# A fixed instruction order revised in a fused agent-attention and feed-forward kernel on one Trainium2 core

## The chip, the core and the metric

The kernel runs on one core of a Trainium2 chip. The metric is the device time of one launch in microseconds (us). The engines are named as in the profile: PE is TensorE (matmuls; PEld its weight loads), DVE is VectorE, ACT is ScalarE, POOL is GpSimd, and SP is SyncE, which issues the DMAs.

## The reference

Four batches of 12,480 rows of 128 go through an attention with 49 agents, and then, as 49,920 tokens, through a feed-forward layer. All is float32.

```python
def _attn_ref(q, k, v, agents):
    scale = 1.0 / np.sqrt(q.shape[-1])
    def sm(a, b):
        s = scale * (a @ b.transpose(0, 2, 1))
        s = s - s.max(-1, keepdims=True)
        e = np.exp(s)
        return e / (e.sum(-1, keepdims=True) + 1e-09)
    agent_v = sm(agents, k) @ v
    return sm(q, agents) @ agent_v

def _moe_ref(x, w_in, w_out):        # w_in: 128 x 2048, w_out: 2048 x 128
    h = x @ w_in
    g = h - np.tanh(h)
    return g @ w_out
```

## The kernel before, in words

The work has two parts, which the kernel runs beside each other.

**The feed-forward part** sets the pace. The product agent_v @ w_in (49 x 2048) is made once per batch, as a rounded part `awh` and a remainder `awl` (`project`, from L433). A batch is cut into 25 blocks of 500 tokens (the last of 480), which makes 100 blocks; two of them are a pair. Each block has eight steps (NCH // 2), each for 256 of the 2048 columns, so there are 800 steps, and sixteen positions (`pos`, 0 to 15) in a pair. For each step:

- the first product `m1` (L528): four matmuls into `h` (L533 with `awh`, L534 with `awl`); `h` has three buffers of two PSUM banks;
- `pre` (L540) on ScalarE: `y` = tanh (L543), then `z` = y squared (L545);
- `mul` (L549) on VectorE: `g` = h times z (L551);
- `high` (L579): `gh`, a rounded copy of `g`, on GpSimd (L584) or, for some steps, on ScalarE (L582);
- `low` (L587) on VectorE: `gl` = g minus gh (L589), the remainder;
- the second product `m2` (L592): six matmuls into the block's accumulator in PSUM, for each of two halves `wo_l` x `gh` (L602), `wo_h` x `gh` (L603), `wo_h` x `gl` (L604). In a plain step (all of block 0, and step PLAIN_PAIR of every even block) there is no `gh` and `gl`, and two float32 matmuls (L600) take their place.

Step k of the loop in `fast` (from L804) issues `squares(k + 1)`, the multiplication and rounding of step k, `low` of step k - 1, the second product of step k - 1, and the first product of step k + AHEAD.

**The attention part** is cut into jobs, which are Python generators. A job that has been started is moved on by one `yield` at the beginning of each step (L822 to L829), so what it issues there stands in front of that step's own multiplication on VectorE and behind the latest square on ScalarE (`hold`, L830).

- A q job (`q_softmax`, L477), one per pair, for the next pair: products of q and the agents (L487), their maximum on VectorE (L494), a copy on ScalarE (L495), the subtraction on GpSimd (L497), exp (L499), sums and division on VectorE (L501 to L504), a rounded copy `pp` on ScalarE (L507) and its remainder on GpSimd (L510). QGAPS says how many steps lie between these. Two jobs `q_transpose` (L515) then make `pT`, the operand of the first product; T0 and T1 are the positions at which they start.
- For the next batch: 13 key jobs (`scores`, L232: products L277, copy to SBUF on ScalarE L279, maximum on VectorE L280), `max_in` and `max_out`, 13 value jobs (`av`, L313: subtraction on GpSimd L321, exp L328, products L336, addition L348), `sums` and four parts of `project`. They start at the positions KS (VS for value jobs), three in a pair. In the step in which a value job starts, the rounding `high` goes to ScalarE, and the job's subtraction waits for that step's multiplication (`wait_for`), so that it takes the rounding's place on GpSimd. At position QLOW the rounding goes to ScalarE too, and the subtraction L510 of the q job, a step later, has its place.

All short PSUM results share two banks (`misc`), of which the running accumulator holds one.

The order on VectorE, GpSimd and TensorE is that in which the program issues the instructions (`issue_order`, L864 to L866). On ScalarE it is written out only up to the end of block 0; after that the compiler's scheduler places the instructions, within what they need and `hold`.

Of the kernel before, what the change touches and what calls it, by code (L numbers as in the profile page):

```python
# [24 lines left out]
A = 49  # L25
# [8 lines left out]
GT = 8  # L34
# [20 lines left out]
LATE = 3  # L55
KV = 3
VB = 4
PLAIN_PAIR = 6
PLAIN_EVERY = 2
NB = dict(y=2, z=2, g=4, gh=4, gl=3)  # L60
Q0 = 2
NV = 10
SPLIT = (8, 9, 11, 13)
AHEAD = 3
QL = 0
QS = 2
QGAPS = (1, 1, 0, 2, 1, 1, 1)
QLOW = 8
T0 = 11
T1 = 13  # L70
KS = (3, 5, 13)
VS = (1, 3, 11)


def width(n):
# [23 lines left out]
class Build:  # L99
# [95 lines left out]
    def phase1(self, b):  # L195
# [30 lines left out]
        def ahead(kind, load, g, depth):  # L226
            have = st.setdefault(kind, [])
            while len(have) < min(NG, g + depth):
                have.append(load(len(have)))
            return have[g]  # L230

        def scores(g):  # L232
            yield
            yield
            if g == 0:
                st["s"] = self.keep.tile([128, NG * (GT + 1) * A], F32, tag="s", name="s", bufs=1)
                if b == 0:
                    st["mxp"] = self.work.tile([128, A, 2 * NG], F32, tag="mxp", name="mxp", bufs=1)
                else:
                    st["mxp"] = st["s"][:, NG * GT * A :][:, : A * NG].rearrange("p (a g) -> p a g", g=NG)  # L240
                st["acc"] = self.small.tile([128, C + 1], F32, tag="acc", name="acc")
            n = tiles(g)
            kt = ahead("k", load_k, g, 1 if b == 0 else kb - 1)
            if b and g >= NG - vb:
                ahead("v", load_v, 0, g - NG + vb + 1)
            if b == 0:
                ps = self.ph.tile([128, 2, 512], F32, tag="h", name="h")
                for t in range(n):
                    nc.tensor.matmul(  # L249
                        ps[:, t // 4, (t % 4) * A2 : (t % 4 + 1) * A2],  # L250
                        kt[:, t, :],
                        self.ag[:, 0:2, :],
                        start=True,
                        stop=True,
                    )
                pv = ps[:, :, : 4 * A2].rearrange("p c (t a) -> p c t a", a=A2)[:, :, :, :A]
                for c in range(-(-n // 4)):
                    m = min(4, n - 4 * c)
                    sl = slice((g * GT + 4 * c) * A, (g * GT + 4 * c + m) * A)
                    nc.scalar.copy(st["s"][:, sl].rearrange("p (t a) -> p t a", a=A), pv[:, c, :m])  # L260
                banks = -(-n // 4)
                nc.vector.tensor_reduce(
                    st["mxp"][:, :, 2 * g : 2 * g + banks].rearrange("p a c -> p c a"),
                    pv[:, :banks, : min(4, n)].rearrange("p c t a -> p c a t"),
                    axis=AX.X,
                    op=ALU.max,
                )
                if g == EARLY - 1:
                    nc.vector.tensor_reduce(
                        st["mxp"][:, :, 2 * NG - 1], st["mxp"][:, :, : 2 * EARLY], axis=AX.X, op=ALU.max  # L270
                    )
                return
            ps = self.misc()
            for t in range(n):
                for r in range(0, 128, QUART):
                    to = ps[r : r + QUART, t * A : (t + 1) * A]
                    nc.tensor.matmul(to, kt[:, t, r : r + QUART], self.ag[:, b, :], start=True, stop=True)  # L277
            yield
            nc.scalar.copy(st["s"][:, g * GT * A : (g * GT + n) * A], ps[:, : n * A])  # L279
            nc.vector.tensor_reduce(  # L280
                st["mxp"][:, :, g],
                ps[:, : n * A].rearrange("p (t a) -> p a t", a=A),
                axis=AX.X,
                op=ALU.max,
            )

        def max_in():
            yield
# [98 lines left out]
        def sums():  # L387
            yield
            yield
            if b == 0:  # L390
                an, n = st["acc"], HALF + A
                nc.vector.tensor_copy(an[:n, :C], st["ps"][:n, :C])
# [32 lines left out]
        if b == 0:  # L425
            self.mb_at = lambda: st["mb_at"]
            self.k0 = lambda g: ahead("k", load_k, g, 1)
            self.v0 = lambda g: ahead("v", load_v, g, 1)
        jobs = [scores(g) for g in range(NG)] + [max_in(), max_out(), None]
        jobs += [av(g) for g in range(NG)] + [None] * (b > 0) + [sums()]  # L430
        return jobs + self.project(b, True)

    def project(self, b, bound):  # L433
        nc = self.nc
# [42 lines left out]
    def q_softmax(self, halves, qt, res, TT=TT, gaps=(1,) * 7):  # L477
# [16 lines left out]
        nc.vector.tensor_reduce(m[:TT], pv, axis=AX.X, op=ALU.max)  # L494
        nc.scalar.copy(ev, pv)  # L495
        yield from (None,) * gaps[2]
        nc.gpsimd.tensor_tensor(ev, ev, m[:TT, :, None].broadcast_to([TT, GT, A]), ALU.subtract)  # L497
        yield from (None,) * gaps[3]
        nc.scalar.activation(ev, ev, AF.Exp, scale=SCALE)  # L499
        yield from (None,) * gaps[4]  # L500
# [91 lines left out]
    def m2(self, acc, i, gh, gl, wf=None):  # L592
        nc = self.nc
        w = gh.shape[1] // 2
        for c in range(2):
            f = 2 * i + c
            x = slice(c * w, (c + 1) * w)
            first, last = f == 0, f == NCH - 1
            if gl is None:
                nc.tensor.matmul(acc[:, :w], wf[:, c * C : (c + 1) * C], gh[:, x], start=first, stop=last)  # L600
                continue
            nc.tensor.matmul(acc[:, :w], self.wo_l[:, f, :], gh[:, x], start=first, stop=False)  # L602
            nc.tensor.matmul(acc[:, :w], self.wo_h[:, f, :], gh[:, x], start=False, stop=False)  # L603
            nc.tensor.matmul(acc[:, :w], self.wo_h[:, f, :], gl[:, x], start=False, stop=last)  # L604

    def last_name(self):
        return self.nc.cur_bb.bb.instructions[-1].name
# [37 lines left out]
    def fast(self):  # L645
# [101 lines left out]
        run(rest0.pop(0))  # L747
        run(dec[0])
        live = []
        kq, nv = [], 0  # L750
        r1, r2, done = [], [], []
        acc, outs, hs, zs = {}, {}, {}, {}

        def start(gen):
            if gen is not None:
                next(gen)
                live.append(gen)
# [17 lines left out]
        def squares(k):  # L775
            if k < len(steps):
                zs[k] = self.pre(hs[k], width(steps[k][0]))
# [26 lines left out]
        for k, (n, i) in enumerate(steps):  # L804
# [2 lines left out]
            p = n // 2  # L807
            if n % NBLK == 0 and i == 0 and b + 1 < B:
                kq = self.phase1(b + 1)
                nv = len(kq) - NG - 1  # L810
            first = self.count()
            while done and done[0][1] < k - 1:
                finish(done.pop(0)[0])
# [14 lines left out]
                    pass  # L828
            live[:] = nxt  # L829
            self.hold(first, self.act_at, (ET.Activation,))  # L830
            squares(k + 1)
            values = nv - NG - 2 < len(kq) < nv
            begin = kq and n and pos in (VS if values else KS)
            by_act = values and begin and kq[0] is not None or p and pos == QLOW and p + 1 < npair
            product(k, by_act)
            low(1)
            mark = self.last_on(ET.DVE)
            if n == 0:
# [10 lines left out]
            out(k)  # L849
            if n == 0 and i == HP - 1:  # L850
                self.issue_order(ET.Activation, at)
            first_product(k + AHEAD)
            if p and p + 1 < npair:
                if pos == QL:
                    qt[p + 1] = self.q_load(q_src(p + 1))
                if pos == QS:
                    start(q_job(p + 1))
            if begin:
                start(kq.pop(0))
        low(0)  # L860
        out(len(steps))
        while done:
# [63 lines left out]
```

## Time and profile before

| | |
|---|---|
| runs | 2222.31, 2222.56, 2222.90 us (median 2222.56) |
| profiled execution | 2226.41 us, span of its instructions 2224.6 us, granted clock 0.996 |
| first multiplication of step 0 | 58.9 us from the span's start |
| last multiplication | 2213.3 us |
| GpSimd roundings (L584) | 656 of 1667 ns |
| ScalarE roundings (L582) | 87 of 1020 ns |

The page of the profile gives each engine's busy time; groups of instructions with their mean duration and the idle time of the engine before them, with what ended it; the waits of one engine for another; and a timeline. In a row such as "DVE s L280 <- ACT s L279: 68.4, 38, 2.6" VectorE's instruction of line 280, which writes the tile s, waited for ScalarE's instruction of line 279: 68.4 us in all, 38 times, at most 2.6. A timeline row has the start in us, the duration in us, the engine, the line, the operation, out<-in, sizes, the number of instructions merged into the row and, in brackets, how long the engine was idle before it and who ended that.

### The profile page before, as it was taken

How to read it: one execution, taken by the hardware profiler on the slowest of the kernel's cores; microseconds unless marked ns; L12 is line 12 of the kernel's file. 1: busy time of each engine (PE TensorE's matmuls, PEld its weight loads, DVE VectorE, ACT ScalarE, POOL GpSimd, SP SyncE). 2: the span in 40 equal slices, each digit the busy share in tenths (PEclk: the TensorE clock that was granted, in tenths of full speed). 3: DMA queues.
4: the chain of work that ended last, by engine and by line, in shares of the span. 5: the costliest groups of instructions: out<-in, count | busy, mean ns of one | idle time of the engine just before them, and what ended most of it. 6: DMA issues, size and time to landing. Idle time of an engine off the chain costs nothing.

```text
span 2224.6 us, 37436 instructions
## 1 busy us (share of the span) xinstructions
PE 2113.7 (95%) x14885; PEld 1627.5 (73%) x14885; DVE 1987.3 (89%) x2028; ACT 1896.3 (85%) x2184; POOL 1340.2 (60%) x809
## 2 busy tenths in 40 slices
PE   7889899999999999999999999999999999999998
PEld 7567677777766767777777667777777777777776
DVE  7888899899988889988998889989999999999998
ACT  3877789998878888999888878898988989989887
POOL 0355566666656556666566556665666766767766
PEclk9999999999999999999999999999999999999999
DMA  9111111211111111112001110121010010000000
GB/s 360 62 58 57 51 37 54 66 52 38 38 45 50 48 50 47 57 50 66 29 19 57 59 49 19 38 67 49 19 34 23 20 37 20 29 29 19 28 10 20
DMA packets 65352, 109.15 MB, mean 49 GB/s; under 512 B 3985, under 2 KB 44177, under 8 KB 65169
## 3 DMA queue, kind: packets, MB, share of 16 engines
q1 hardware_dynamic: 65168, 106.68, 14.6%
q8 instruction: 119, 1.95, 0.4%
q14 instruction: 65, 0.52, 0.1%
HBM read 81.10 MB, written 25.56 MB: 48 GB/s over the span
## 4 chain that ended last, share of the span: by engine, by line
PE 69%; DVE 13%; ACT 12%; issue 4%; POOL 2%; DMA 0%; POOLq 0%; SPq 0%; DVEq 0%; ACTq 0%
PE misc L604 13%; PE h L534 13%; PE h L533 13%; PE misc L602 12%; PE misc L603 11%; DVE gl L589 6%; ACT y L543 5%; DVE g L551 4%; ACT z L545 4%; PE misc L600 3%; PE misc L336 2%; POOL gh L584 1%; PE h L249 1%; PE misc L520 1%; DVE s L280 1%
## 5 line engine op out<-in xcount | busy, mean ns | idle before, releaser
L584 POOL TENSOR_SCALAR gh<-g 128x1000 fp32r<-128x1000 f32 (+1 forms) x656 | 1091.9, 1667 | 669.2 <-DVE g L551 633.9
L551 DVE TENSOR_TENSOR g<-h,z 128x1000 f32<-128x1000 f32 (+1 forms) x800 | 952.0, 1192 | 53.7 <-ACT z L545 45.3
L543 ACT ACTIVATE y<-h 128x1000 f32<-128x1000 f32 (+1 forms) x800 | 803.1, 1004 | 221.1 <-PE h L534 214.4
L589 DVE TENSOR_TENSOR gl<-g,gh 128x1000 fp32r<-128x1000 f32 (+1 forms) x743 | 927.0, 1248 | 35.4 <-POOL gh L584 29.0
L545 ACT ACTIVATE z<-y 128x1000 f32<-128x1000 f32 (+1 forms) x800 | 833.2, 1042 | 21.6 <-DVE g L551 0.8
L604 PE MATMUL misc<-gl,wo_h 128*128 128x500 f32 (+1 forms) x1486 | 602.1, 405 | 89.3 <-DVE gl L589 89.1
L533 PE MATMUL h<-pT,awh 98*128 98x500 f32 (+1 forms) x1600 | 644.8, 403 | 3.2 <-ACT awh L453 1.5
L534 PE MATMUL h<-pT,awl 98*128 98x500 f32 (+1 forms) x1600 | 623.2, 390 | 0.4 <-DVE awl L456 0.4
L602 PE MATMUL misc<-gh,wo_l 128*128 128x500 f32 (+1 forms) x1486 | 599.2, 403 | 0.0
L603 PE MATMUL misc<-gh,wo_h 128*128 128x500 f32 (+1 forms) x1486 | 577.1, 388 | 0.0
L604 PEld LDWEIGHTS misc<-gl,wo_h 128*128 128x128 f32 x1486 | 279.4, 188 | 229.4 <-DVE gl L589 175.1
L533 PEld LDWEIGHTS h<-pT,awh 98*128 98x128 f32 x1600 | 301.5, 188 | 79.2 <-issue 12.5
L534 PEld LDWEIGHTS h<-pT,awl 98*128 98x128 f32 x1600 | 304.0, 190 | 73.5 <-issue 11.3
L603 PEld LDWEIGHTS misc<-gh,wo_h 128*128 128x128 f32 x1486 | 281.3, 189 | 50.1 <-issue 2.2
L602 PEld LDWEIGHTS misc<-gh,wo_l 128*128 128x128 f32 x1486 | 279.9, 188 | 48.8 <-issue 6.6
L497 POOL TENSOR_TENSOR qe<-qe,qm 126x392 f32<-126x392 f32 x50 | 82.2, 1644 | 122.5 <-ACT qe L495 122.5
L510 POOL TENSOR_TENSOR pp<-qe,pp 126x392 fp32r<-126x392 f32 x50 | 91.5, 1830 | 54.5 <-DVE g L551 45.4
L582 ACT CAST gh<-g 128x1000 fp32r<-128x1000 f32 x87 | 88.8, 1020 | 5.7 <-DVE g L551 5.6
L600 PE MATMUL misc<-g,wo_f 128*128 128x500 f32 (+1 forms) x196 | 93.0, 596 | 0.0
L321 POOL TENSOR_TENSOR s<-s,mb 128x392 f32<-128x392 f32 (+1 forms) x39 | 70.3, 1803 | 29.3 <-DVE g L551 29.3
L280 DVE TENSOR_REDUCE s<-misc 128x49 f32<-128x392 f32 (+1 forms) x39 | 21.2, 544 | 68.4 <-ACT s L279 68.4
L765 ACT ACTIVATE o<-misc 128x500 f32<-128x500 f32 (+1 forms) x100 | 57.5, 575 | 21.4 <-PE misc L604 20.7
(104 smaller groups left out, 869.1 us busy)
## 6 DMA issues: line engine op xcount, KB each, us to landing
kt<-kT SPq DMA_DIRECT2D x48, 512.0 KB, 3.9
qt<-qT SPq DMA_DIRECT2D x46, 500.0 KB, 3.6
outT<-o SPq DMA_DIRECT2D x46, 500.0 KB, 2.6
v<-v SPq DMA_DIRECT2D x36, 512.0 KB, 4.0
vt<-v SPq DMA_DIRECT2D x12, 512.0 KB, 7.0
raw<-w_in SPq DMA_DIRECT2D x4, 512.0 KB, 9.1
v<-w_out SPq DMA_DIRECT2D x4, 512.0 KB, 8.0
qt<-qT SPq DMA_DIRECT2D x4, 490.0 KB, 3.4
```

Source lines behind the costliest of these rows:

```text
L510: nc.gpsimd.tensor_tensor(pp[:TT, :, A:], ev, pp[:TT, :, :A].bitcast(F32), ALU.subtract)
L533: nc.tensor.matmul(h[:, c, :w], aw[0][:A2, sl], pT[:A2, :w], start=True, stop=False)
L534: nc.tensor.matmul(h[:, c, :w], aw[1][:A2, sl], pT[:A2, :w], start=False, stop=True)
L543: nc.scalar.activation(self.pair(y), h, AF.Tanh, scale=TSC)
L545: nc.scalar.activation(z, y, AF.Square)
L551: self.nc.vector.tensor_tensor(self.pair(g), h, self.pair(z), ALU.mult)
L584: self.nc.gpsimd.tensor_scalar(gh, g, 1.0, 0.0, ALU.mult, ALU.add)
L589: self.nc.vector.tensor_tensor(gl, g, gh.bitcast(F32), ALU.subtract)
L600: nc.tensor.matmul(acc[:, :w], wf[:, c * C : (c + 1) * C], gh[:, x], start=first, stop=last)
L602: nc.tensor.matmul(acc[:, :w], self.wo_l[:, f, :], gh[:, x], start=first, stop=False)
L603: nc.tensor.matmul(acc[:, :w], self.wo_h[:, f, :], gh[:, x], start=False, stop=False)
L604: nc.tensor.matmul(acc[:, :w], self.wo_h[:, f, :], gl[:, x], start=False, stop=last)
```

## The change

Seven edits to the order; no arithmetic of the fast path is different but for which step of an even block is plain and the order in which six products are added.

- In `scores`, the maximum is issued in front of the copy; as both read one PSUM bank, the second waits for the first.
- The first product of step k + 2 is issued right behind step k's jobs; before it was the first product of step k + 3 at the end of step k.
- In `q_softmax`, the subtraction comes one step later than the copy and waits for the latest multiplication; the exp and all behind it come a step later too.
- Roundings on ScalarE: positions 4 and 9 of each pair in place of 8.
- In `m2`, the two `gl` matmuls stand behind the four `gh` matmuls.
- The plain step of an even block is its last (7) instead of 6.
- Start positions: T0, T1, the last of KS and of VS are one later; `max_in`, `max_out`, `sums` and `project` start at positions 3 and 5 only, and `sums` waits three steps more.

```diff
-PLAIN_PAIR = 6
+PLAIN_PAIR = NCH // 2 - 1
-AHEAD = 3
+AHEAD = 2
-QGAPS = (1, 1, 0, 2, 1, 1, 1)
-QLOW = 8
-T0 = 11
-T1 = 13
-KS = (3, 5, 13)
-VS = (1, 3, 11)
+QGAPS = (1, 1, 1, 2, 1, 1, 1)
+QACT = (4, 9)
+T0 = 12
+T1 = 14
+KS = (3, 5, 14)
+VS = (1, 3, 12)
+OS = (3, 5)
@@ scores
-            nc.scalar.copy(st["s"][:, g * GT * A : (g * GT + n) * A], ps[:, : n * A])
             nc.vector.tensor_reduce(
...
             )
+            nc.scalar.copy(st["s"][:, g * GT * A : (g * GT + n) * A], ps[:, : n * A])
@@ sums
             yield
             yield
+            if b:
+                yield
+                yield
+                yield
@@ end of phase1
+        if b:
+            jobs = [(KS, scores(g)) for g in range(NG)] + [(OS, max_in()), (OS, max_out())]
+            jobs += [(VS, av(g)) for g in range(NG)]
+            return jobs + [(OS, job) for job in [sums(), None] + self.project(b, True)]
@@ q_softmax
+        first = self.count()
         nc.gpsimd.tensor_tensor(ev, ev, m[:TT, :, None].broadcast_to([TT, GT, A]), ALU.subtract)
+        if gaps != (1,) * 7:
+            self.wait_for(first, self.mul_at)
@@ m2
+        for f, x in parts:
+            nc.tensor.matmul(acc[:, :w], self.wo_l[:, f, :], gh[:, x], start=f == 0, stop=False)
             nc.tensor.matmul(acc[:, :w], self.wo_h[:, f, :], gh[:, x], start=False, stop=False)
-            nc.tensor.matmul(acc[:, :w], self.wo_h[:, f, :], gl[:, x], start=False, stop=last)
+        for f, x in parts:
+            nc.tensor.matmul(acc[:, :w], self.wo_h[:, f, :], gl[:, x], start=False, stop=f == NCH - 1)
@@ fast
             self.hold(first, self.act_at, (ET.Activation,))
+            first_product(k + AHEAD)
             squares(k + 1)
-            values = nv - NG - 2 < len(kq) < nv
-            begin = kq and n and pos in (VS if values else KS)
-            by_act = values and begin and kq[0] is not None or p and pos == QLOW and p + 1 < npair
-            product(k, by_act)
+            begin = kq and n and pos in kq[0][0]
+            values = begin and kq[0][0] is VS
+            product(k, values or p and pos in QACT and p + 1 < npair)
...
             if n == 0 and i == HP - 1:
                 self.issue_order(ET.Activation, at)
-            first_product(k + AHEAD)
```

More of the change, by code (lines that the diff above doesn't have):

```diff
@@ L428, in phase1 @@
             self.v0 = lambda g: ahead("v", load_v, g, 1)
+        if b:
+            jobs = [(KS, scores(g)) for g in range(NG)] + [(OS, max_in()), (OS, max_out())]
+            jobs += [(VS, av(g)) for g in range(NG)]
+            return jobs + [(OS, job) for job in [sums(), None] + self.project(b, True)]
         jobs = [scores(g) for g in range(NG)] + [max_in(), max_out(), None]
-        jobs += [av(g) for g in range(NG)] + [None] * (b > 0) + [sums()]
-        return jobs + self.project(b, True)
+        return jobs + [av(g) for g in range(NG)] + [sums()] + self.project(b, True)
     def project(self, b, bound):
@@ L594, in m2 @@
         w = gh.shape[1] // 2
[L595 to L602, printed above, removed]
+        parts = [(2 * i + c, slice(c * w, (c + 1) * w)) for c in range(2)]
+        if gl is None:
+            for c, (f, x) in enumerate(parts):
+                nc.tensor.matmul(acc[:, :w], wf[:, c * C : (c + 1) * C], gh[:, x], start=f == 0, stop=f == NCH - 1)
+            return
+        for f, x in parts:
+            nc.tensor.matmul(acc[:, :w], self.wo_l[:, f, :], gh[:, x], start=f == 0, stop=False)
             nc.tensor.matmul(acc[:, :w], self.wo_h[:, f, :], gh[:, x], start=False, stop=False)
-            nc.tensor.matmul(acc[:, :w], self.wo_h[:, f, :], gl[:, x], start=False, stop=last)
+        for f, x in parts:
+            nc.tensor.matmul(acc[:, :w], self.wo_h[:, f, :], gl[:, x], start=False, stop=f == NCH - 1)
     def last_name(self):
@@ L749, in fast @@
         live = []
-        kq, nv = [], 0
+        kq = []
         r1, r2, done = [], [], []
@@ L809, in fast @@
                 kq = self.phase1(b + 1)
-                nv = len(kq) - NG - 1
             first = self.count()
@@ L858, in fast @@
             if begin:
-                start(kq.pop(0))
+                start(kq.pop(0)[1])
         low(0)
```

## The prediction

> **What bounds the kernel now.** I read the page first, then the windows of three pairs of blocks, the waits, and the timeline inside those pairs. The page names TensorE.
>
> ```profile
> PE 2113.7 (95%) x14885; PEld 1627.5 (73%) x14885; DVE 1987.3 (89%) x2028; ACT 1896.3 (85%) x2184; POOL 1340.2 (60%) x809
> ```
>
> Records of matmuls and of VectorE overlap, so I take each engine's pace from starts in the timeline. A step (eight to a block, sixteen to a pair) is one tile of 128 x 1000.
>
> ```profile
> 1943.71 1.19 DVE L589 TENSOR_TENSOR gl<-g,gh 128x1000 fp32r<-128x1000 f32 x1
> 1943.92 0.40 PE L533 MATMUL h<-pT,awh 98*128 98x500 f32 x1
> ...
> 1945.30 0.39 PE L604 MATMUL misc<-gl,wo_h 128*128 128x500 f32 x1
> ...
> 1946.20 0.40 PE L533 MATMUL h<-pT,awh 98*128 98x500 f32 x1
> ```
>
> ```profile
> 1263.22 1.19 DVE L589 TENSOR_TENSOR gl<-g,gh 128x1000 fp32r<-128x1000 f32 x1
> ...
> 1265.44 1.19 DVE L589 TENSOR_TENSOR gl<-g,gh 128x1000 fp32r<-128x1000 f32 x1
> ...
> 1274.37 1.01 ACT L543 ACTIVATE y<-h 128x1000 f32<-128x1000 f32 x1 [0.83 <-PE h L534]
> ...
> 1276.35 0.52 ACT L499 ACTIVATE qe<-qe 126x392 f32<-126x392 f32 x1
> ```
>
> With nothing else to do TensorE needs 2.28 us a step (1943.92 to 1946.20, ten matmuls), VectorE 2.22 (gl to gl), ScalarE 1.98 (tanh at 1274.37, square, next instruction at 1276.35). The three are within 0.3 us of each other and tied in a ring: gl feeds the second product, then comes the next first product, its tanh and square, and the multiplication that stands two places later on VectorE. In a quiet step a gl ends at 1943.71 + 1.19 = 1944.90 and TensorE uses it at 1945.30: a margin of 0.40 us. Whatever delays VectorE or ScalarE by more stops TensorE.
>
> Three pairs, each cut from the start of its first multiplication to the next pair's, with three key (score) groups, three value groups, and neither:
>
> ```profile
> 1262.10:1308.96 46.86, 42.59 (x424) 32.54 (x423) 39.14 (x40) 37.95 (x43) 26.95 (x16) 1.00 0.18 57
> 1483.90:1527.06 43.16, 42.80 (x279) 32.83 (x278) 38.69 (x40) 39.41 (x47) 26.85 (x16) 1.00 0.20 61
> 1938.02:1978.29 40.27, 39.07 (x232) 30.63 (x231) 37.97 (x37) 36.06 (x40) 27.21 (x17) 1.00 0.08 27
> ```
>
> (Columns: length, then busy time of PE, PEld, DVE, ACT, POOL.) A key group costs (46.86 - 40.27) / 3 = 2.20 us. The value pair leaves ScalarE little: 39.41 of 43.16 busy. The waits say where key groups lose:
>
> ```profile
> ACT y L543 <- PE h L534: 214.4, 432, 1.7
> ...
> PE misc L604 <- DVE gl L589: 89.1, 106, 1.6
> DVE s L280 <- ACT s L279: 68.4, 38, 2.6
> ...
> DVE qm L494 <- PE misc L487: 31.4, 34, 2.3
> ...
> DVE acc L348 <- PE misc L336: 16.3, 24, 0.8
> ```
>
> TensorE idles for gl (89.1 us); VectorE in turn waits for ScalarE's copy of the scores (68.4), for the q products (31.4) and the value products (16.3).
>
> **Part A, key maximum before the copy.**
>
> ```profile
> 1305.91 0.90 PE L277 MATMUL misc<-ag,kt 128*32 128x49 f32 x64
> 1306.01 1.00 ACT L543 ACTIVATE y<-h 128x1000 f32<-128x1000 f32 x1 [0.20 <-PE h L534]
> ...
> 1307.05 1.04 ACT L545 ACTIVATE z<-y 128x1000 f32<-128x1000 f32 x1
> 1307.99 0.47 ACT L279 COPY s<-misc 128x392 f32<-128x392 f32 x1
> 1308.49 0.57 DVE L280 TENSOR_REDUCE s<-misc 128x49 f32<-128x392 f32 x1 [2.59 <-ACT s L279]
> 1308.98 1.19 DVE L551 TENSOR_TENSOR g<-h,z 128x1000 f32<-128x1000 f32 x1
> ```
>
> The scores are there at about 1306.8; the maximum runs at 1308.49, because the copy comes first and stands behind a tanh and a square. Turned round, the maximum follows the products directly. Of the 2.20 us the products keep about 1.0 (0.90 and a start), so 1.2 goes. 39 groups x 1.2 = **-47 us**. At most the whole wait goes, 68.4. The new wait is the copy's: behind it on ScalarE is the next tanh, and if that always waits for the maximum (0.57), 39 x (1.2 - 0.57) = 25 is left of the gain. I take the upper value, because ScalarE waits for its first product anyway (214.4 us) and the copy fits into that gap. The Trainium skill, PSUM — Partial Sum Buffer, section "PSUM bank collisions raise a hardware error", says that two engines may not use one bank at once, reads included; by that the wait is not removed but turned round, and A would be about -25 us. The rows above agree that the two do not overlap (the copy ends at 1308.46, the maximum starts at 1308.49); no row of before shows the copy second.
>
> **Part B, the q subtraction in a rounding's place.**
>
> ```profile
> 1948.18 0.57 DVE L494 TENSOR_REDUCE qm<-misc 126x8 f32<-126x392 f32 x1 [0.83 <-PE misc L487]
> ...
> 1949.77 1.19 DVE L589 TENSOR_TENSOR gl<-g,gh 128x1000 fp32r<-128x1000 f32 x1
> 1949.85 1.81 POOL L497 TENSOR_TENSOR qe<-qe,qm 126x392 f32<-126x392 f32 x1 [1.62 <-ACT qe L495]
> ...
> 1950.88 1.19 DVE L551 TENSOR_TENSOR g<-h,z 128x1000 f32<-128x1000 f32 x1
> ...
> 1951.63 2.04 POOL L584 TENSOR_SCALAR gh<-g 128x1000 fp32r<-128x1000 f32 x2
> ...
> 1952.70 2.01 DVE L589 TENSOR_TENSOR gl<-g,gh 128x1000 fp32r<-128x1000 f32 x1 [0.63 <-POOL gh L584]
> ...
> 1954.64 1.19 DVE L551 TENSOR_TENSOR g<-h,z 128x1000 f32<-128x1000 f32 x1
> 1954.77 0.50 PE L604 MATMUL misc<-gl,wo_h 128*128 128x500 f32 x1 [1.20 <-DVE gl L589]
> ```
>
> The subtraction takes GpSimd just when a rounding is due. The rounding starts at 1951.63, gl waits 0.63 and then runs 2.01 instead of 1.19 beside the next rounding: VectorE loses 0.63 + 0.82 = 1.45, TensorE idles 1.20. After the change step 4's rounding goes to ScalarE, and the subtraction waits for that step's multiplication and takes the free place. The pp subtraction stands in such a place already:
>
> ```profile
> 1960.77 1.20 DVE L589 TENSOR_TENSOR gl<-g,gh 128x1000 fp32r<-128x1000 f32 x1
> 1960.81 1.98 POOL L510 TENSOR_TENSOR pp<-qe,pp 126x392 fp32r<-126x392 f32 x1
> ```
>
> gl keeps its 1.20 there, and only GpSimd waits. Pairs 1 to 48 have it; 13 value groups, three a pair, fill four pairs in each of three batches, 12 in all. I remove 1.45 in the other 36 and, since PE is idle for only 43.16 - 42.80 = 0.36 us of the value pair, 0.4 in the 12: 36 x 1.45 + 12 x 0.4 = **-57 us**; its bounds are 48 x 1.45 = 70 and 36 x 0.63 = 23 (the plain wait alone). The added wait holds the next step's rounding behind the subtraction, which has a step's time for 1.81.
>
> **Part C, ScalarE pays.** Two roundings a pair (steps 4 and 9) replace one (step 8).
>
> ```profile
> L582 ACT CAST gh<-g 128x1000 fp32r<-128x1000 f32 x87 | 88.8, 1020 | 5.7 <-DVE g L551 5.6
> ```
>
> 48 more of 1.02 us are 49 us of ScalarE. A step spares 2.28 - 1.98 = 0.30. In step 4 the q copy (as large as the 0.47 copy above) and the rounding come to 1.49 - 0.30 = 1.19 behind; in step 9 the pp cast and the rounding to about the same. The margin becomes 0.40 + 0.45 (next part) = 0.85, so 0.34 shows at each, 0.7 a pair; value pairs, with roundings in steps 1, 3 and 4, I put at 1.2. 36 x 0.7 + 12 x 1.2 = **+40 us**; between 0 (all of it hidden by the products that stop TensorE at step 3) and 98 (48 x 2 x 1.02, all shown).
>
> **Part D, gl terms last, and jobs' products in front.** No instruction is added. The first gl term moves behind two matmuls of 2.28 / 10 us each: gl may come 0.45 later. Besides the idle that B removes, each pair has small lateness:
>
> ```profile
> PEld misc L604 <- DVE gl L589: 2.6, 4, 1.6
> ...
> PE misc L604 <- DVE gl L589: 1.2, 1, 1.2
> ```
>
> (Waits of the pair without groups.) Of the 2.6 - 1.2 = 1.4 that the weight loads alone waited I take 0.4: 48 x 0.4 = **-19 us**, from 0 to -67. A product in front of a first product is ready 0.9 us sooner (four matmuls), so VectorE's 31.4 and 16.3 us of waiting go; the first product and its tanh come later by the product's length. As everything behind it on TensorE comes later by the same, I cost this at nothing; its cover is that VectorE's own job instruction fills the time. First and second products keep their order: product k + 3 was issued at the end of step k and is now issued in step k + 1, with only that step's jobs before it. There are 57 plain steps as before; as the last step of a block, a plain one spares VectorE its gl in step 8, where the q sums are now, as step 6 did for step 7. Moving T0, T1, KS and VS by one keeps the distance to their users; the SP loads that key and value jobs issue move with them by a step.
>
> **Part E, small change.** max_out's product now stands before a first product and needs VectorE's dg of the same step: three times about 0.9, the four matmuls that covered it. The projections, two a pair instead of three, end later but before their first use. **+3 us**.
>
> **Sum.** -47 - 57 + 40 - 19 + 3 = -80. The profiled execution took 2226.41 us (span 2224.6 and 1.8 around it), so it would take 2146; the median of the runs shown is 2222.56, 3.9 less, and I take the same difference off that: **2143 us**.
>
> **Rivals.** (1) ScalarE shows all of C (+98 in place of +40) and D gives nothing: 2222.6 - 47 - 57 + 98 + 3 = 2220 at the worst, and about 2181 half way from the forecast, where I put it. For it: 39.41 of 43.16 in value pairs; against it: 214.4 us of ScalarE's waits for TensorE. (2) VectorE is the bound and every wait taken from it comes off: 68.4 + 31.4 + 16.3 = 116, 2106. For it: 2.22 a step plus its jobs; against it: TensorE's 2.28. The Trainium skill, Perfetto Trace Analysis, section "Identifying the Most-Contended Engine", calls matmul busy time a poor measure and ranks the other engines by occupancy; by it VectorE's 89% stands first, which the starts above do not bear out. (3) A's wait is handed to ScalarE: 39 x 0.57 = 22 more, 2165. (4) Slower: products in front of a first product starve ScalarE. They are
>
> ```profile
> L487 PE MATMUL misc<-ag,qt 128*32 128x49 f32 (+1 forms) x3200 | 45.0, 208 | 0.0
> L336 PE MATMUL misc<-v,s 128*49 128x129 f32 (+2 forms) x588 | 41.7, 279 | 0.0
> L520 PE MATMUL misc<-identr,pp 126*98 126x126 f32 x400 | 41.6, 227 | 1.7 <-POOL pp L510 1.7
> ...
> L277 PE MATMUL misc<-ag,kt 128*32 128x49 f32 x2352 | 33.6, 209 | 0.0
> ```
>
> 45.0 + 41.7 + 41.6 + 33.6 = 162 us. If all of it became idle of ScalarE that is never made up, the time is 2143 + 162 = 2305; it turns the sign once half of it (80 us) shows, if ScalarE is the engine in the way at most of these places. Against it: TensorE's later work moves by the same. (5) The two orders come to the same because ScalarE's own order, which is not written out in the main loop, puts copy and roundings where they are late: 2222.
>
> **How the numbers follow.** Forecast 0.50 (2120 to 2163, for B and D between their ends); rival 1 0.22; rival 2 0.13; rival 3 0.07; rival 4 0.05; rival 5 0.03. Faster by over 0.2% (about what a measurement of this kernel can tell from no change) is 0.50 + 0.22 + 0.13 + 0.07 = 0.92, same 0.03, slower 0.05. The range runs from just under rival 2 to a little beyond rival 1's half way: 2103 to 2188.
>
> **What would show it.** Right: the wait of the maximum for the copy is gone (under 5 us of 68.4), a key pair takes 41.5 to 43 us, a plain pair 38.7 to 39.5, a value pair 42 to 43.5; gl beside the q subtraction lasts 1.2; TensorE's wait for gl falls from 89 to under 30; ScalarE has 135 roundings. Wrong: gl waits for ScalarE's roundings (3.0 us now) by tens of us, tanh waits longer for its product than 214 us, or the copy holds up the tanh behind it.

## The result, and the profile after

The changed kernel takes 2146.11 us (median of 4 runs, 2144.79 to 2147.12) against 2222.73 for the one before (4 runs): a ratio of 0.9654, with a 95% interval of 0.9637 to 0.967. The forecast was 2143. The profiled execution took 2144.79 us, its span 2143.0, at a granted clock of 0.997 (0.996 before). The total hides that several terms of the sum were wrong by about 40 us each. I start with what the profile shows.

From the page of the changed kernel, the engines' busy time and three of the groups:

```profile
PE 2085.6 (97%) x14885; PEld 1632.7 (76%) x14885; DVE 1960.8 (91%) x2028; ACT 1918.9 (90%) x2232; POOL 1312.3 (61%) x761
...
L600 DVE TENSOR_TENSOR gl<-g,gh 128x1000 fp32r<-128x1000 f32 (+1 forms) x743 | 906.4, 1220 | 9.5 <-ACT gh L593 4.8
...
L593 ACT CAST gh<-g 128x1000 fp32r<-128x1000 f32 (+1 forms) x135 | 138.6, 1026 | 0.0
L506 POOL TENSOR_TENSOR qe<-qe,qm 126x392 f32<-126x392 f32 x50 | 81.6, 1631 | 83.5 <-ACT qe L503 42.3
```

The 48 roundings moved to ScalarE are there (135 for 87). The gl takes 1220 ns in the mean, and it hardly waits for a rounding (4.8 us). The list of waits of the changed kernel:

```profile
DVE g L562 <- ACT z L556: 134.7, 177, 1.5
ACT y L554 <- PE h L545: 101.2, 243, 1.5
...
PE misc L615 <- DVE gl L600: 35.6, 57, 1.2
ACT s L286 <- DVE s L280: 9.3, 12, 1.1
```

The three waits of VectorE from which the prediction started (68.4, 31.4 and 16.3 us) are gone, and TensorE waits 35.6 us for gl in place of 89.1. VectorE's largest wait is now another: its multiplication waits 134.7 us for ScalarE's square. Before, the same wait was small:

```profile
DVE g L551 <- ACT z L545: 45.3, 116, 1.1
...
DVE gl L589 <- POOL gh L584: 29.0, 50, 0.9
```

The same three pairs as in the prediction (three key groups, three value groups, neither); the columns are the window, its length, and the busy time of PE, PEld, DVE, ACT and POOL:

```profile
1207.50:1250.40 42.90, 41.91 (x424) 32.91 (x424) 38.48 (x39) 38.01 (x45) 26.93 (x16) 1.00 0.20 62
1418.47:1462.83 44.36, 42.72 (x280) 32.92 (x279) 39.28 (x39) 39.94 (x49) 25.12 (x16) 1.00 0.19 59
1865.37:1904.20 38.83, 38.78 (x231) 30.71 (x231) 36.81 (x36) 36.80 (x42) 26.92 (x16) 1.00 0.08 27
```

The key pair lost 46.86 - 42.90 = 3.96 us and the pair without groups 1.44, to TensorE busy for 38.78 of 38.83. The value pair, for which the prediction said 42 to 43.5, became longer: 44.36 for 43.16.

One key group in the changed kernel's timeline (start, duration, engine, line):

```profile
1209.01 0.90 PE L278 MATMUL misc<-ag,kt 128*32 128x49 f32 x64
...
1209.97 0.57 DVE L280 TENSOR_REDUCE s<-misc 128x49 f32<-128x392 f32 x1
...
1210.58 0.48 ACT L286 COPY s<-misc 128x392 f32<-128x392 f32 x1 [0.74 <-DVE s L280]
...
1211.05 1.01 ACT L554 ACTIVATE y<-h 128x1000 f32<-128x1000 f32 x1
```

The maximum follows the products at once, and the copy goes between it and the next tanh, as part A said. One value group and what stands round it, from the same kernel's timelines of ScalarE and VectorE, in order of time:

```profile
1424.29 1.02 ACT L593 CAST gh<-g 128x1000 fp32r<-128x1000 f32 x1
...
1425.20 1.01 ACT L554 ACTIVATE y<-h 128x1000 f32<-128x1000 f32 x1
...
1425.35 2.04 DVE L600 TENSOR_TENSOR gl<-g,gh 128x1000 fp32r<-128x1000 f32 x1 [0.20 <-ACT gh L593]
...
1426.40 1.00 ACT L554 ACTIVATE y<-h 128x1000 f32<-128x1000 f32 x1 [0.19 <-PE h L545]
...
1427.30 1.96 ACT L556 ACTIVATE z<-y 128x1000 f32<-128x1000 f32 x2
...
1428.37 1.20 DVE L562 TENSOR_TENSOR g<-h,z 128x1000 f32<-128x1000 f32 x1 [0.99 <-ACT z L556]
```

ScalarE runs two tanhs (1425.20, 1426.40) and only then both squares (two in one row, from 1427.30). The multiplication of the first of the two steps wants the first square alone; it stands idle for 0.99 us. The gl before it starts late, behind the rounding, and takes 2.04 in place of 1.19 beside a GpSimd rounding that runs from 1425.31. Had the square followed its tanh, it would have been ready about 1.1 us sooner (1426.21 + 1.04 = 1427.25, where it was at about 1428.34). This order is the scheduler's; the program fixes none between these instructions of ScalarE. In the changed kernel's ScalarE rows 36 tanhs are directly followed by another tanh, and 81 of the 135 roundings stand directly between a tanh and a square. Before it was 2 tanhs and 15 roundings.

Where the time came from, by kind of pair, mean length in us (12 pairs with three key groups, 12 with three value groups, the last 11 with neither, and the other 14), with the medians of the kernels below:

| kernel | key | value | neither | other | median us | ratio to before, 95% |
|---|---|---|---|---|---|---|
| before | 47.15 | 43.23 | 40.21 | 42.40 | 2222.73 | |
| after | 42.68 | 44.16 | 38.75 | 40.76 | 2146.11 | 0.9654 (0.9637-0.967) |
| e6, before + maximum first | 42.71 | 43.22 | 40.21 | 42.17 | 2169.44 | 0.9746 (0.973-0.9763) |
| e12, before + products in front | 41.44 | 44.25 | 38.47 | 41.21 | 2134.46 | 0.9605 (0.9589-0.9621) |
| e1, after with copy first | 42.63 | 44.16 | 38.75 | 40.84 | 2143.67 | 0.9637 (0.962-0.9654) |
| e2, after with q part as before | 41.28 | 43.25 | 39.27 | 41.00 | 2124.93 | 0.9551 (0.9534-0.9569) |
| e3, after with gl between | 43.14 | 45.14 | 39.52 | 41.22 | 2178.20 | 0.9794 (0.9777-0.9811) |
| e4, after with products behind | 41.42 | 42.28 | 38.64 | 40.66 | 2105.36 | 0.9465 (0.9448-0.9482) |
| e9, e4 with copy first | 43.17 | 42.28 | 38.64 | 41.04 | 2130.64 | 0.9574 (0.9558-0.959) |
| e10, e4 with q part as before | 42.75 | 42.54 | 41.18 | 42.68 | 2179.24 | 0.9793 (0.9777-0.9809) |
| e13, e4 with gl between | 42.62 | 42.68 | 39.20 | 41.61 | 2142.95 | 0.9643 (0.9627-0.9659) |
| e7, after + ScalarE's order | 41.81 | 42.08 | 38.63 | 40.71 | 2107.90 | 0.9471 (0.9455-0.9487) |
| e14, e7 with q part as before | 41.28 | 41.82 | 39.27 | 40.81 | 2106.41 | 0.948 (0.9464-0.9495) |
| e11, e4 + ScalarE's order | 41.43 | 41.98 | 38.64 | 40.79 | 2103.20 | 0.946 (0.9444-0.9477) |

The experiments were run in three groups (e1 to e4; e6, e7, e9, e10; e11 to e14), each beside the kernel before, whose medians there were 2223.73, 2226.98 and 2221.66; the changed kernel itself ran apart from them, beside 2222.73. Each ratio is known to about 0.0017, or 3.8 us, so a difference between kernels of two groups is uncertain by about 5 us (3.8 times the root of 2).

### The profile page after: what moved, and what is told of

The parts are those of the page before. It is cut to its first block, busy times and chain, and to the rows that moved or that the text cites. A ratio compares the mean times of both kernels' runs of the same rounds, so it can differ in the third digit from the quotient of the medians.

```text
span 2143.0 us, 37562 instructions
## 1 busy us (share of the span) xinstructions
PE 2085.6 (97%) x14885; PEld 1632.7 (76%) x14885; DVE 1960.8 (91%) x2028; ACT 1918.9 (90%) x2232; POOL 1312.3 (61%) x761
## 4 chain that ended last, share of the span: by engine, by line
PE 69%; DVE 16%; ACT 8%; issue 5%; DMA 1%; POOL 0%; SPq 0%; ACTq 0%; POOLq 0%; DVEq 0%
PE h L544 14%; PE misc L615 13%; PE h L545 13%; PE misc L612 11%; PE misc L613 11%; DVE gl L600 7%; DVE g L562 5%; ACT z L556 4%; PE misc L609 3%; ACT y L554 2%; PE misc L337 2%; PE misc L278 1%; PE misc L531 1%; PE h L250 1%; PE misc L495 1%
## 5 line engine op out<-in xcount | busy, mean ns | idle before, releaser
L595 POOL TENSOR_SCALAR gh<-g 128x1000 fp32r<-128x1000 f32 (+1 forms) x608 | 1060.6, 1744 | 663.9 <-DVE g L562 609.1
L562 DVE TENSOR_TENSOR g<-h,z 128x1000 f32<-128x1000 f32 (+1 forms) x800 | 951.8, 1192 | 144.4 <-ACT z L556 134.7
L600 DVE TENSOR_TENSOR gl<-g,gh 128x1000 fp32r<-128x1000 f32 (+1 forms) x743 | 906.4, 1220 | 9.5 <-ACT gh L593 4.8
L554 ACT ACTIVATE y<-h 128x1000 f32<-128x1000 f32 (+1 forms) x800 | 801.6, 1002 | 106.2 <-PE h L545 101.2
L544 PE MATMUL h<-pT,awh 98*128 98x500 f32 (+1 forms) x1600 | 670.2, 419 | 2.6 <-ACT awh L461 1.4
L612 PE MATMUL misc<-gh,wo_l 128*128 128x500 f32 (+1 forms) x1486 | 576.1, 388 | 0.5 <-POOL gh L595 0.3
L615 PE MATMUL misc<-gl,wo_h 128*128 128x500 f32 (+1 forms) x1486 | 469.1, 397 | 37.6 <-DVE gl L600 35.6
L615 PEld LDWEIGHTS misc<-gl,wo_h 128*128 128x128 f32 x1486 | 265.8, 188 | 133.2 <-DVE gl L600 87.6
L593 ACT CAST gh<-g 128x1000 fp32r<-128x1000 f32 (+1 forms) x135 | 138.6, 1026 | 0.0
L506 POOL TENSOR_TENSOR qe<-qe,qm 126x392 f32<-126x392 f32 x50 | 81.6, 1631 | 83.5 <-ACT qe L503 42.3
L536 ACT CAST pT<-misc 98x500 fp32r<-98x500 f32 (+1 forms) x100 | 56.1, 562 | 14.2 <-PE misc L531 14.2
```

Source lines behind the costliest of these rows:

```text
L544: nc.tensor.matmul(h[:, c, :w], aw[0][:A2, sl], pT[:A2, :w], start=True, stop=False)
L554: nc.scalar.activation(self.pair(y), h, AF.Tanh, scale=TSC)
L562: self.nc.vector.tensor_tensor(self.pair(g), h, self.pair(z), ALU.mult)
L593: self.nc.scalar.copy(gh, g)
L595: self.nc.gpsimd.tensor_scalar(gh, g, 1.0, 0.0, ALU.mult, ALU.add)
L600: self.nc.vector.tensor_tensor(gl, g, gh.bitcast(F32), ALU.subtract)
```

## The experiments

**e1: the copy first again.** Theory: part A is worth what the prediction gave it. Rival: something else in the change already removes the wait.

```diff
+            nc.scalar.copy(st["s"][:, g * GT * A : (g * GT + n) * A], ps[:, : n * A])
             nc.vector.tensor_reduce(
...
-            nc.scalar.copy(st["s"][:, g * GT * A : (g * GT + n) * A], ps[:, : n * A])
```

> The kernel after with the copy in front of the key maximum again. Prediction's part A: 47 us come back, about 2193, key pairs 42.8 -> about 46.4 us, VectorE waits for the copy again (about 68 us); other pairs unchanged. Rival 2 (VectorE is the bound): the whole 68 us, about 2214. Rival 3 (the wait was handed to ScalarE): 25 us, about 2171.

Measured: 2143.67 us, 2.4 less than the change. A is worth nothing here. A key group in e1's timeline shows why:

```profile
1208.23 0.90 PE L278 MATMUL misc<-ag,kt 128*32 128x49 f32 x64
...
1209.20 0.49 ACT L280 COPY s<-misc 128x392 f32<-128x392 f32 x1
...
1209.72 0.57 DVE L281 TENSOR_REDUCE s<-misc 128x49 f32<-128x392 f32 x1 [0.58 <-ACT s L280]
...
1210.28 1.01 ACT L554 ACTIVATE y<-h 128x1000 f32<-128x1000 f32 x1 [0.58 <-PE h L545]
```

The copy comes first, but no tanh stands in front of it: the first product of that tanh is now issued behind the scores, so the scores are ready before it, and ScalarE is free when they are. The maximum is late by the copy's 0.49 us alone.

**e2: the q part as before.** The subtraction in its old place, without its wait, and one rounding at position 8 instead of 4 and 9: parts B and C undone together.

```diff
-QGAPS = (1, 1, 1, 2, 1, 1, 1)
-QACT = (4, 9)
+QGAPS = (1, 1, 0, 2, 1, 1, 1)
+QACT = (8,)
-        if gaps != (1,) * 7:
-            self.wait_for(first, self.mul_at)
```

> The kernel after with the q subtraction in its old place (same step as the copy, no wait) and one ScalarE rounding a pair (position 8) instead of two. Parts B and C: B's 57 come back and C's 40 go, so about 2163; pairs without groups 38.75 -> about 39.9 us, value pairs 44.2 -> about 43 us, gl beside the subtraction lasts 2.0 us again. Rival (ScalarE's second rounding costs nothing, C = 0): 2203. Rival 1 (C is all of 98): 2105.

Measured: 2124.93, 21 us faster. Parts B and C together cost 21 us in the change, where the prediction had them gain 57 - 40 = 17 (e14 shows what else this edit touches). The subtraction's row in e2, and one of its q parts:

```profile
L506 POOL TENSOR_TENSOR qe<-qe,qm 126x392 f32<-126x392 f32 x50 | 42.5, 850 | 55.7 <-ACT qe L503 55.7
```

```profile
2050.54 0.85 POOL L506 TENSOR_TENSOR qe<-qe,qm 126x392 f32<-126x392 f32 x1 [0.18 <-ACT qe L503]
...
2050.96 1.48 DVE L598 TENSOR_TENSOR gl<-g,gh 128x1000 fp32r<-128x1000 f32 x1
2051.36 1.98 POOL L593 TENSOR_SCALAR gh<-g 128x1000 fp32r<-128x1000 f32 x1
```

In its old place it lasts 850 ns, against 1631 after. The q products stand in front of a first product as well, so maximum, copy and subtraction come earlier. The subtraction starts ahead of a gl and not within one; the rounding behind it starts 0.32 us after its multiplication has ended (2049.85 + 1.19 = 2051.04), where in the kernel before that was 1.78 us (the median), and gl takes 1.48, where in the prediction's rows it took 2.01. Most of the disturbance that B was to remove is gone without B.

**e3: the gl terms between again.**

```diff
-        for f, x in parts:
             nc.tensor.matmul(acc[:, :w], self.wo_h[:, f, :], gl[:, x], start=False, stop=f == NCH - 1)
```

(The last matmul goes back into the first loop, so each half's gl term stands behind its two gh terms.)

> The kernel after with the gl matmuls between the gh matmuls again. Part D: 19 us come back, about 2165, and TensorE's wait for gl rises from 36 us by about as much. If gl's margin of 0.45 us is also what pays for the ScalarE roundings (C without it), 48 x 2 x 0.45 = 43 more, about 2189. Rival 2 (VectorE is the bound): no change, 2146.

Measured: 2178.20, 32 us slower. From e3's waits:

```profile
DVE g L562 <- ACT z L556: 190.5, 274, 1.5
...
PE misc L614 <- DVE gl L600: 57.7, 112, 1.6
```

TensorE waits 57.7 us for gl in place of 35.6. Part D is real, and larger than 19.

**e4: the first product late again.** The first product of step k + 3 at the end of step k, so that jobs' products stand behind it.

```diff
-AHEAD = 2
+AHEAD = 3
-            first_product(k + AHEAD)
             squares(k + 1)
...
+            first_product(k + AHEAD)
```

> The kernel after with the first product at the end of the step again (AHEAD 3), behind the second product, so that jobs' products stand behind it. Prediction: no change, 2146 within 5 us, though VectorE waits for q and value products again (31 + 16 us). Rival 2 (VectorE is the bound): 47 us come back, 2193. Rival 4 (products in front starve ScalarE): faster than 2146, by up to 80.

Measured: 2105.36, 41 us faster than the whole change. The edit that the prediction held to be free costs 41 us beside the other six. From e4's waits, and its three pairs:

```profile
DVE g L562 <- ACT z L556: 55.6, 116, 1.1
...
DVE qm L502 <- PE misc L495: 32.7, 48, 0.9
...
DVE s L280 <- PE misc L278: 18.7, 26, 1.0
...
DVE acc L349 <- PE misc L337: 15.8, 24, 0.7
```

```profile
1180.98:1222.42 41.44, 41.44 (x424) 32.90 (x423) 38.20 (x40) 38.27 (x44) 26.73 (x16) 1.00 0.21 64
1387.10:1429.40 42.30, 42.28 (x280) 33.11 (x279) 37.71 (x39) 39.97 (x48) 26.80 (x16) 1.00 0.21 62
1826.62:1865.32 38.70, 38.57 (x232) 30.90 (x231) 36.80 (x37) 36.79 (x41) 26.87 (x16) 1.00 0.08 28
```

VectorE again waits for the products of jobs (32.7 + 18.7 + 15.8 = 67 us), and no cost of it shows: TensorE's records cover all of 41.44, 42.28 of 42.30, and 38.57 of 38.70. TensorE has almost no idle time left in these pairs. VectorE's wait for the square is back near its old size (55.6). With the first product late, 12 tanhs are followed by a tanh, and 10 roundings stand directly between a tanh and a square.

**e6: the maximum first, alone, on the kernel before.** Theory: about -47, as part A says. Rival: the copy's own wait gives most of it back.

```diff
-            nc.scalar.copy(st["s"][:, g * GT * A : (g * GT + n) * A], ps[:, : n * A])
             nc.vector.tensor_reduce(
...
+            nc.scalar.copy(st["s"][:, g * GT * A : (g * GT + n) * A], ps[:, : n * A])
```

> The kernel before with the key maximum in front of the copy and nothing else. New theory (either edit, this one or the products in front, takes the wait of 68 us away, and in the kernel after each hides the other): 47 to 68 us gained, 2155 to 2176, key pairs 47.15 -> about 43.5 us, other pairs unchanged. Rival (the order of maximum and copy is worth nothing, as undoing it in the kernel after showed): 2223.

Measured: ratio 0.9746 (0.973 to 0.9763), 57 us off, where the prediction put 47. Nearly all of it is in the key pairs: 47.15 - 42.71 = 4.44 in each of 12 is 53 us. TensorE's wait for gl went from 89.1 to 40.5 with this edit alone, and VectorE now waits a little for the products themselves:

```profile
PE misc L604 <- DVE gl L589: 40.5, 76, 1.6
...
DVE s L279 <- PE misc L277: 16.8, 25, 1.0
```

**e7: ScalarE's order written out.** On the changed kernel, each tanh is held behind the square before it, and a rounding on ScalarE behind the latest square and ahead of the next tanh. Nothing else differs; `hold` gives an order on one engine and no semaphore. (A line that sets `act_at` to None at the start is not printed here.)

```diff
@@ pre
+        at = self.count()
         nc.scalar.activation(self.pair(y), h, AF.Tanh, scale=TSC)
+        if self.act_at:
+            self.hold(at, self.act_at, (ET.Activation,))
...
@@ high
         if act:
+            at = self.count()
             self.nc.scalar.copy(gh, g)
+            self.hold(at, self.act_at, (ET.Activation,))
+            self.act_at = self.last_name()
```

> The kernel after with ScalarE's order written out: each tanh behind the square before it, each ScalarE rounding behind the latest square and in front of the next tanh. In the kernel after a rounding stands between a tanh and its square 81 times and two tanhs follow each other 36 times. Theory (that order is what the products in front and the roundings cost): value pairs 44.2 -> about 42.5 us, VectorE's wait for z 135 -> under 60 us, time 2105 to 2125. Rival (the later first product itself costs, whatever the order): 2146 within 5 us.

Measured: 2107.90, 38 us faster than the change, with the same instructions and the products still in front. The same stretch of the value pair in e7's timelines of ScalarE and VectorE:

```profile
1393.77 1.01 ACT L598 CAST gh<-g 128x1000 fp32r<-128x1000 f32 x1
...
1395.01 1.19 DVE L607 TENSOR_TENSOR gl<-g,gh 128x1000 fp32r<-128x1000 f32 x1
...
1395.16 1.00 ACT L556 ACTIVATE y<-h 128x1000 f32<-128x1000 f32 x1
...
1396.19 1.04 ACT L560 ACTIVATE z<-y 128x1000 f32<-128x1000 f32 x1
```

The rounding comes ahead of the output copy, gl starts when it is done and lasts 1.19, and each tanh has its square behind it. The value pairs fall from 44.16 to 42.08. So the 41 us that products in front cost came by way of ScalarE's order, and not by ScalarE starving for its first product: e7 keeps the products in front and has that gain too. One expectation failed: the multiplication's wait for the square fell to 113.6 us, not under 60. TensorE's wait for gl fell from 35.6 to 9.3, so the size of VectorE's wait is no measure of what the order cost.

**e9: e4 with the copy first.** Part A where the products stand behind. On e4:

```diff
@@ scores
+            nc.scalar.copy(st["s"][:, g * GT * A : (g * GT + n) * A], ps[:, : n * A])
             nc.vector.tensor_reduce(
...
-            nc.scalar.copy(st["s"][:, g * GT * A : (g * GT + n) * A], ps[:, : n * A])
```

> The kernel with the first product at the end of the step (2105 us) and the copy in front of the maximum again. New theory (the two edits hide each other): the wait for the copy is back, 47 to 68 us, 2152 to 2173, all in key pairs. Rival (the order of maximum and copy is worth nothing): 2105.

Measured: 2130.64, 25 us over e4. The wait that A removes is there again (52.3 us, at most 2.6):

```profile
DVE s L281 <- ACT s L280: 52.3, 38, 2.6
```

Of the 47 to 68 us expected, 25 come back; TensorE's wait for gl rises only from 5.4 to 18.7. Why A is worth less here than in e6 was not tested.

**e10: e4 with the q part as before.** Parts B and C where the products stand behind. On e4:

```diff
-QGAPS = (1, 1, 1, 2, 1, 1, 1)
-QACT = (4, 9)
+QGAPS = (1, 1, 0, 2, 1, 1, 1)
+QACT = (8,)
-        if gaps != (1,) * 7:
-            self.wait_for(first, self.mul_at)
```

> The kernel with the first product at the end of the step (2105 us), and the q subtraction in its old place with one ScalarE rounding a pair. Theory (the second rounding costs only where it comes between a tanh and its square; with the first product late that is 10 times instead of 81): the collision of parts B comes back and little is saved, 2110 to 2160. Rival (the new place costs 21 us as it does with products in front): 2084.

Measured: 2179.24, 74 us over e4, more than the 2110 to 2160 expected; the prediction's B and C come to 17. Waits, and the group of the subtraction, of e10:

```profile
PE misc L613 <- DVE gl L598: 54.1, 82, 2.2
...
DVE gl L598 <- POOL gh L593: 30.0, 48, 0.9
```

```profile
L506 POOL TENSOR_TENSOR qe<-qe,qm 126x392 f32<-126x392 f32 x50 | 86.8, 1735 | 115.9 <-ACT qe L503 107.4 <-DMA qt<-qT 8.5
```

The subtraction is slow again and gl waits 30.0 us for GpSimd's rounding behind it; in e2, with products in front and the same q part, that wait is 1.6. Not all of the 74 us is the subtraction's (see e14).

**e11: e4 with ScalarE's order written out.** On e7:

```diff
-AHEAD = 2
+AHEAD = 3
-            first_product(k + AHEAD)
             squares(k + 1)
...
+            first_product(k + AHEAD)
```

> The kernel with the first product at the end of the step (2105 us), and ScalarE's order written out as in e7. Theory (what an order written out gains is the two tanhs in a row and the roundings between a tanh and its square; here 12 and 10 times instead of 36 and 81): a gain of 0 to 12 us, 2093 to 2105. Rival (a written order is worth 38 us wherever it stands): 2067.

Measured: 2103.20, the fastest of all, though only 2 us from e4. With the products behind, the scheduler's own order was already nearly this one; e11 is also within the uncertainty of e7.

**e12: products in front, alone, on the kernel before.**

```diff
-AHEAD = 3
+AHEAD = 2
             self.hold(first, self.act_at, (ET.Activation,))
+            first_product(k + AHEAD)
             squares(k + 1)
...
-            first_product(k + AHEAD)
```

> The kernel before with the first product right behind the jobs (AHEAD 2) and nothing else. Prediction: worth nothing, 2223. New theory (jobs' products in front of a first product take away both VectorE's wait for the copy and the q subtraction's meeting with gl, by bringing both forward): subtraction about 0.85 us instead of 1.64, no wait of the maximum for the copy, 2223 less some 50 to 90 us, 2130 to 2170. Rival 4 of the prediction (products in front starve ScalarE): slower than 2223.

Measured: ratio 0.9605 (0.9589 to 0.9621), 87 us off: this one edit brings more than all seven together. Its waits, and its group of the subtraction:

```profile
DVE g L551 <- ACT z L545: 82.5, 146, 1.8
...
DVE s L280 <- ACT s L279: 16.8, 28, 0.8
...
DVE gl L589 <- POOL gh L584: 2.9, 4, 0.9
```

```profile
L497 POOL TENSOR_TENSOR qe<-qe,qm 126x392 f32<-126x392 f32 x50 | 42.6, 852 | 59.9 <-ACT qe L495 51.4 <-DMA qt<-qT 8.5
```

It has neither A nor B, and it removes what each was for: the maximum's wait for the copy falls from 68.4 to 16.8, the subtraction lasts 852 ns, and gl's wait for GpSimd falls from 29.0 to 2.9. It also shows the cost: the wait for the square rises from 45.3 to 82.5, and the value pairs from 43.23 to 44.25.

**e13: e4 with gl between.** Part D where the products stand behind. On e4:

```diff
-        for f, x in parts:
             nc.tensor.matmul(acc[:, :w], self.wo_h[:, f, :], gl[:, x], start=False, stop=f == NCH - 1)
```

> The kernel with the first product at the end of the step (2105 us), and the gl matmuls between the gh matmuls again. Prediction's part D: 19 us come back, 2124. As in the kernel after: 32 us, 2137. Theory that gl last only pays for ScalarE's bad order, which is rarer here: under 10 us, 2105 to 2115.

Measured: 2142.95, 38 us over e4. Part D is worth 32 to 38 in both surroundings.

**e14: e7 with the q part as before.** Parts B and C with ScalarE's order written out. On e7:

```diff
-QGAPS = (1, 1, 1, 2, 1, 1, 1)
-QACT = (4, 9)
+QGAPS = (1, 1, 0, 2, 1, 1, 1)
+QACT = (8,)
-        if gaps != (1,) * 7:
-            self.wait_for(first, self.mul_at)
```

> e7 (ScalarE's order written out, 2108 us) with the q subtraction in its old place and one ScalarE rounding a pair. Theory (with products in front the subtraction does not meet gl, so its new place gains nothing and 49 us of ScalarE's work go): value pairs 42.1 or less, time 2085 to 2108. Rival (the new place is worth 74 us, as it is with the first product late): about 2180.

Measured: 2106.41, against 2107.90 of e7: no difference in the sum. So the 21 us by which B and C lengthen the change are gone from the sum once ScalarE's order is written out. By kind of pair, the new q part still costs 0.53 us in key pairs (41.81 for 41.28) and 0.26 in value pairs, and gains 0.64 in pairs without groups.

That gain is not the subtraction's. e2, e10 and e14 put the q part back but leave the plain step at 7. The q sums then stand in step 7 again, in front of that step's multiplication and the gl of step 6. With plain step 6, as in the kernel before and in e12, there is no such gl. A pair without groups of e12, one of e2, and the place in the second at which TensorE idles:

```profile
1779.67:1818.18 38.51, 38.51 (x232) 30.86 (x231) 37.38 (x37) 36.18 (x40) 28.02 (x17) 1.00 0.08 28
```

```profile
1765.32:1804.56 39.24, 38.46 (x232) 30.89 (x231) 37.55 (x37) 36.39 (x40) 27.93 (x17) 1.00 0.08 27
```

```profile
1786.19 0.72 PE L613 MATMUL misc<-gl,wo_h 128*128 128x500 f32 x2 [0.78 <-DVE gl L598]
```

At this place TensorE idles for 12.6 us in all in e2 and in e14 (16 pairs), and for 29.0 in e10 (24 pairs). By an estimate that takes all of it off, B and C cost about 13 us beside e7, about 34 in the change, and gain about 45 beside e4. A kernel with the plain step put back as well was not run.

e2 against e14 also shows a price of two tanhs in a row. In e2 each of the 12 value pairs has them once, and no rounding stands directly between a tanh and a square. With the order written out the value pairs fall by 1.43 us (43.25 to 41.82), the other kinds by 0.19 or less.

## Why the prediction was right in the sum and wrong in its terms

The step that failed is in part D, on the jobs' products: "As everything behind it on TensorE comes later by the same, I cost this at nothing; its cover is that VectorE's own job instruction fills the time." It holds for TensorE's order alone. It leaves out two things. First, a score that is ready before the next first product meets an idle ScalarE, and the same holds for q: this edit alone gains 87 us (e12), by the very waits for which A and B were made. Second, with the later tanh the scheduler chose another order on ScalarE, where nothing is written out; that costs 41 beside the other edits (after against e4), and 38 of it come back when the order is written out (e7).

Point by point:

- **Part A, -47.** Alone it is -57 (e6): right in mechanism, a little small, since a group saved 4.44 / 3 = 1.48 us where I took 1.2. In the change it is worth nothing (e1), and with the products behind 25 (e9 against e4). The Trainium skill, PSUM — Partial Sum Buffer, section "PSUM bank collisions raise a hardware error", says that two engines may not use one bank at once, and I had put the gain by that rule at 25. The rows after agree that the two stay apart (maximum to 1210.54, copy from 1210.58), but ScalarE's wait for the maximum is 9.3 us in all, not 39 x 0.57 = 22, and A alone gives more than twice the 25.
- **Part B, -57, and part C, +40.** Measured together: -74 with the products behind (e10), +21 in the change (e2), 0 with ScalarE's order written out (e14); without the plain step's share, by the estimate at e14, about -45, +34 and +13. The sum of -17 is none of these. What B describes did happen: gl beside the moved subtraction takes 1.19 us, and gl's wait for GpSimd is 1.6 us in e4 where it is 30.0 in e10. With the products behind, the estimate of 45 lies between the 17 and B's 57. C's 0.7 a pair is not seen in the pairs without groups: e7, with two ScalarE roundings in each, needs 38.63, and e12, with one, 38.47.
- **Part D, gl last, -19.** It is -32 (e3) and -38 (e13): right in mechanism; I gave it about half of what it is.
- **The sum.** Without the products in front, the change is e4, 2105.36, 118 us under before; the same terms in the prediction made 80. A, B, C and D were 38 too small together, and the products in front, put at 0, cost 41. The two errors cancel by luck, and the forecast of 2143 stands beside 2146 for that reason alone.

The signs that the prediction named came out in part. Key pairs (42.68) and pairs without groups (38.75) lie in the bounds given, the ScalarE roundings are 135, the maximum's wait is gone, and gl waits for ScalarE's roundings for 4.8 us. The value pair is out of bounds (44.16 for 42 to 43.5) and TensorE's wait for gl is 35.6 where under 30 was said.

The rivals:

- The first (all of C shows, D gives nothing) fails on both terms: D gave 32 to 38, and B and C together cost 21, about 34 by the estimate at e14, where C alone was to cost 98.
- The second named a time, 2106, that the best kernels reach, but not for its reason: e4 keeps 67 us of VectorE's waits for products, and e7, without them, is not faster. The Trainium skill, Perfetto Trace Analysis, section "Identifying the Most-Contended Engine", calls matmul busy time no good measure of how close TensorE is to its peak, and ranks VectorE and ScalarE by occupancy. The trace agrees with the first half: TensorE's records cover 42.28 us of a value pair of 42.30 in e4, and a value pair of e14 takes 41.94. By the second half VectorE stands first in e4 (92%), and its waits there cost nothing that shows.
- The third (A's wait handed to ScalarE, A worth 25) is excluded on the kernel before, where A alone gives 57 (e6).
- The fourth said that products in front starve ScalarE, and would have had e4 faster than the change by up to 80. e4 is 41 faster, but not for that reason: the tanh's wait for its product fell from 214.4 to 101.2 with the change, and e7 gains 38 with the products still in front.
- The fifth, ScalarE's unwritten order, was taken to undo everything and given little weight; it was there, at about 38 us.

Three things stay open. The new start positions were not tried apart from the rest, nor was the plain step, of which only the idle shown at e14 is known. The two disorders on ScalarE were not separated in one kind of pair: two tanhs in a row cost 1.43 us in a value pair of e2, but in e4, which has them once in each value pair too, the written order takes off only 0.30 (e11). A rounding before a square, alone, stands once in each of the changed kernel's last 11 pairs, which are 0.12 longer than those of e7. And the three added steps of `sums` have no price of their own.

## What to carry to other kernels

Edits that each remove a wait in one ring of engines aren't added up. Here A was worth 57 us, and B with C 74 (about 45 by the estimate), where nothing else took their place, and no part of it once an earlier product had removed the same lateness. Price each edit with the others in place, and take back with it what was set to suit it, as the plain step here. Gains end near the engine that has almost no idle time left: four different kernels take 2103 to 2108 us. Of an instruction that is moved on one engine, ask what becomes ready before what on the next engine, and whether the order there is written down: if a scheduler chooses it, two instructions that change places can cost as much as the edit gains.

## What the runs showed of the hardware

The same subtraction on GpSimd (126 x 392, two inputs) takes 850 to 852 ns in the mean in e2 and e12, and 1631 to 1735 ns in the changed kernel and e10. In the latter two 48 of the 50 start while a gl runs on VectorE; in e2 none does. In the changed kernel the gl is not lengthened:

```profile
2070.04 1.19 DVE L600 TENSOR_TENSOR gl<-g,gh 128x1000 fp32r<-128x1000 f32 x1
...
2070.27 1.66 POOL L506 TENSOR_TENSOR qe<-qe,qm 126x392 f32<-126x392 f32 x1 [0.84 <-DVE g L562]
```

The gl from 2070.04 ends at 2071.23, and 0.85 us later would be 2072.08; the subtraction ends at 2071.93. So it waits out the rest of the gl, or nearly. The Trainium skill, SBUF — State Buffer, section "Who interferes with whom", says that a VectorE instruction with two inputs in SBUF shuts out a GpSimd read until it is done, and that the one issued first decides; these rows agree to within 0.15 us. In e2's rows the order is the other way round: the subtraction from 2050.54 keeps its 0.85, and the gl that starts in it takes 1.48 in place of 1.19. Had it waited for the subtraction's end at 2051.39, it would have ended at 2052.58; it ended at 2052.44.
